# Linear attention and MLP on one core: two loads of tokens issued sooner, one GpSimd subtraction held back behind a norm, and one tile's sums in another order

## The chip, the core and the metric

The kernel runs on one core of a Trainium2 chip. The metric is the device time of one execution in microseconds (us); lower is better. TensorE (PE) multiplies matrices, VectorE (DVE), ScalarE (ACT) and GpSimd (POOL) work element by element, and SyncE (SP) issues nearly all DMAs, in the order in which they stand in the program. An engine works through its own instructions strictly in order, and so does SP: an instruction that waits holds up all that stand behind it.

## The reference

```
xn  = layernorm(x)                               x: 2048 x 512, float32
qkv = xn @ wqkv                                  32 heads of 16
pq, pk = phi(q), phi(k)                          phi(t) = (t + 1 if t > 0 else exp(t)) + 1e-6
kv  = sum over tokens of pk^T v,  z = sum over tokens of pk
o   = (pq kv) / (pq z + 1e-6)
A   = o @ wo
B   = relu(xn @ w1 + b1)^2 @ w2 + b2             hidden size 1376
out = x + A + B
```

## The kernel before, in words

The 2048 tokens are 16 tiles of 128. All matrix products are kept near float32 by splitting each operand into a high part (rounded to float32r) and a low part (the rest), and by three passes: high by high, high by low, low by high.

The first stage goes over the tiles in order. For tile `i`:

- `load_x` (line 157) brings its rows of x. Tiles 0 to 3 come singly, 4 to 7 with one DMA, 8 to 15 in pairs of 512 KB each. The buffers of tiles 12 and 13 are those of tiles 0 and 1 (`two("x12")`), those of 14 and 15 are those of 2 and 3.
- `measure` (L230, L231) takes mean and variance on VectorE, `roots` (L241, L242) makes the reciprocal root on GpSimd with a power (the tile `power` holds the exponent), and `normalise` writes the normalised tile `xp`: on VectorE (L264) for tiles 0 to 7, on ScalarE (L254) from tile 8 on.
- The tile has to be transposed for the projection. Tiles 0 to 3 are transposed on TensorE (L304). From tile 4 on it goes through memory: `regroup` (line 273) stores `xp` to a buffer `via` (L277) as soon as the tile is normalised, and appends four gathers to the list `moves`; `move` (L285) issues them, which brings `xg`; then VectorE's block transpose (L289) finishes the turn. Tiles 4 and 5 have a `via` and a gather each (`xg4s`, 256 KB), later tiles go in pairs (512 KB).
- ScalarE makes the high part of the transposed tile (L320), VectorE the low part (L323). For tiles up to 7 the transposed tile is also kept in memory (`xTd`, L332).
- `project` (L365) multiplies it by the key weights: 12 matmuls into the bank `pk`. `phi_k` applies phi (ScalarE L356 and L358, VectorE L360), and `parts` splits the result (ScalarE L111 for the high part, VectorE L373 for the low one). `tokens` splits the normalised tile itself into `tok` (ScalarE L111 high, GpSimd L119 low).
- `kx` (L385) adds tokens times keys into four banks: 12 matmuls, three passes of four. Its order is a table by tile: for the first tiles high tokens by high keys, then low tokens by high keys, then high tokens by low keys; from tile 2 on the low tokens come last.

Tiles 0 to 3 are written out by hand, line by line (lines 515 to 649), with the loads of tiles 8 to 11 placed behind tile 2's steps. The loop over `i` from 2 to 15 (line 788 on) then issues, per turn: the gathers in `moves`; in turn 2 the loads of tiles 12 to 15; in turns 4 and 7 a copy of a block of transposed tiles to memory (`xsd`, two DMAs of 1 MB, L802); the projection of tile `i`; phi; the norm of the tiles two or more ahead with its `via`; the splits; the statistics further ahead; and last `kx(i - 1)`. So on TensorE the order is projection of tile 3, sums of tile 2, projection of tile 4, sums of tile 3, and so on.

For tiles 0 to 2 the order on the other engines is by hand too. Around the change VectorE does: phi of tile 0 (L360), statistics of tile 4, low keys of tile 0 (L373), phi of tile 1, norm of tile 4 (L264), statistics of tile 5, low keys of tile 1 (L373), then the low part of tile 3 (L323) and so on. GpSimd does: low tokens of tile 0 (L119), root of tile 4 (L241, L242), low tokens of tile 1 (L119), root of tile 5. SP does: `xTd` of tiles 0 and 1, loads of 8/9 and 10/11, `via` of tile 4, `xTd` of tile 2, four gathers of tile 4, loads of 12/13 and 14/15, `via` of tile 5, `xTd` of tile 3, four gathers of tile 5, `via` of tiles 6 and 7, `xTd` of 4 and 5, four gathers of 6 and 7, and the two copies of 1 MB.

After this stage the values and the query projection are folded into matrices, and two large rounds of matmuls follow (L130, L484), which take most of the time.

Of the kernel before, what the change touches and what calls it, by code (L numbers as in the profile page):

```python
# [7 lines left out]
F32 = mybir.dt.float32  # L8
# [5 lines left out]
P = 128  # L14
# [4 lines left out]
def kernel(  # L19
# [30 lines left out]
    nc = tc.nc  # L50
# [21 lines left out]
    keep = ctx.enter_context(tc.tile_pool(name="keep", bufs=1))  # L72
# [8 lines left out]
    def w512(name, tag, bufs):  # L81
        return work.tile([P, 512], F32, name=name, tag=tag, bufs=bufs)
# [3 lines left out]
    def next_tag(of):  # L86
        k, n = turns[of]
        turns[of][0] = (k + 1) % n
        return f"{of}{k}"

    def two(name):
        return keep.tile([P, 2, 512], F32, name=name, tag=next_tag("x"))
# [4 lines left out]
    def pair(name):  # L97
        return keep.tile([P, 2, 512], F32R, name=name, tag=next_tag("pair"))

    def f32(ap):  # L100
        return ap.bitcast(F32)

    def gjc(ap):

        return ap.rearrange("p (j g c) -> p g j c", j=NJ, g=NJ)
# [3 lines left out]
    def copy(eng, o, i, bias=0.0):  # L109
        if eng == "act":  # L110
            nc.scalar.activation(o, i, AF.Copy, bias=bias)  # L111
        elif bias:
            ENG[eng].tensor_scalar(o, i, bias, None, op0=OP.add)
        else:
            ENG[eng].tensor_copy(o, i)

    def split(h, l, src, eh, el):
        copy(eh, h, src)
        ENG[el].tensor_tensor(out=l, in0=src, in1=f32(h), op=OP.subtract)  # L119
# [30 lines left out]
    heads = work.tile([P, P], F32, name="heads", tag="heads")  # L150
    b1s = keep.tile([P, NF], F32, name="b1s")
    zc = keep.tile([P, 2, NJ], F32, name="zc")
    power = keep.tile([P, 3], F32, name="power")

    xr, xp, xg, tok, pk, kp = {}, {}, {}, {}, {}, {}

    def load_x(i, t):
        n = t.shape[1]
        nc.sync.dma_start(t, xf[i * P:(i + n) * P, :].rearrange("(i p) d -> p i d", i=n))
        for k in range(n):  # L160
            xr[i + k] = t[:, k]
# [82 lines left out]
    def normalise(tiles, st, mv, y):  # L244

        n = len(tiles)
        r, u = (y[:, k, :n] for k in range(2))
        if tiles[-1] >= NPE:

            nc.vector.scalar_tensor_tensor(u, mv[:, :n, 0], -1.0, r, op0=OP.mult, op1=OP.mult)  # L250
        later = []

        def last(i, o, src, k):
            nc.scalar.activation(o, src, AF.Identity, bias=u[:, k:k + 1], scale=r[:, k:k + 1])  # L254
            if i in groups:
                regroup(i)

        for k, i in enumerate(tiles):
            o, src = xp[i], xr[i]
            if i >= NDVE:  # L260

                o, src = o.rearrange("p g (j c) -> p g j c", j=NJ), gjc(src)
            if i < NPE:
                nc.vector.tensor_scalar(o, src, mv[:, k, 0:1], r[:, k:k + 1], op0=OP.subtract, op1=OP.mult)  # L264
                if i in groups:
                    regroup(i)
            else:
                later.append(lambda a=(i, o, src, k): last(*a))
        return later
# [3 lines left out]
    def regroup(i):  # L273

        src, G = groups[i]
        via = dram.tile([P, NJ, src.shape[-1]], F32, name=f"via{i}")
        nc.sync.dma_start(via, src)  # L277
        of_g = via.rearrange("(r t) g n -> g t r n", r=NJ)
        for g in range(NJ):
            moves.append((G[32 * g:32 * (g + 1)], of_g[g]))  # L280
# [11 lines left out]
    def slot(i):  # L292
        return slice((i % TB) * P, (i % TB + 1) * P)

    def cols(i):

        return xsb[(i // TB + 1) % 2]
# [42 lines left out]
    def ones(i):  # L340

        nc.gpsimd.memset(xp[i][:, D - 1:] if i < NDVE else xp[i][:, NJ - 1, P - 1:], 1.0)

    def tokens(i):
        tok[i] = pair(f"tok{i}")
        h, l = tok[i][:, 0], tok[i][:, 1]
        src = xp[i]
        if i >= NDVE:
            h, l, src = gjc(h), gjc(l), src.rearrange("p g (j c) -> p g j c", j=NJ)
        split(h, l, src, "act", "pool")  # L350
        if NDVE <= i + 1 < NT:
            ones(i + 1)
# [9 lines left out]
    def project(i, ps, w, steps, first=True, last=True):  # L362

        for n, (j, u, v) in enumerate(steps):
            nc.tensor.matmul(ps, lhsT=cols(i)[u][:, j, slot(i)], rhs=w[v][:, j, :], start=first and n == 0,  # L365
                             stop=last and n == len(steps) - 1)

    def parts(i):

        p = kp[i]  # L370
        pk[i] = pair(f"pk{i}")
        copy("act", pk[i][:, 0], p, 1e-6)
        nc.vector.scalar_tensor_tensor(pk[i][:, 1], p, 1e-6, f32(pk[i][:, 0]), op0=OP.add, op1=OP.subtract)  # L373

    def phi_k(i, ps, mid=lambda: None, late=lambda: None):
        kp[i] = w512(f"k{i}", "p", 6)
        phi(ps, kp[i], mid, late)

    def kx(i):
        second, third = ((1, 0), (0, 1)) if i < 2 else ((0, 1), (1, 0))  # L380
        order = (((1, 0),), ((0, 0), (0, 1))) if i >= NPE else (((0, 0),), (second,), (third,))
        todo = [(c, u, v) for group in order for c in range(NJ) for u, v in group]
        first, last = order[0][0], order[-1][-1]
        for c, u, v in todo:
            nc.tensor.matmul(kxp[c], lhsT=tok[i][:, u, c * P:(c + 1) * P], rhs=pk[i][:, v],  # L385
                             start=i == 0 and (u, v) == first, stop=i == NT - 1 and (u, v) == last)
# [152 lines left out]
    for i0 in range(0, NT, TB):  # L539
# [6 lines left out]
        if i0 < NPE:  # L546
            single = work.tile([P, 2, 512], F32, name=f"xg{i0}s", tag="r0")
            for k in range(2):
                i = i0 + k
# [3 lines left out]
        for k in range(0, n, 2):  # L553
            i = i0 + TB - n + k
# [51 lines left out]
    third = statistics(2)  # L606
# [25 lines left out]
    rest(3)  # L632
    load_x(8, x8[:, :2])
    load_x(10, x8[:, 2:])
    project(2, pks[2], wk, HL)
    single = group(4)
    soon = group(5)
# [4 lines left out]
    roots(*single)  # L642
    parts(0)
    phi_k(1, pks[1])
    tokens(1)
    normalise(*single)
    measure(soon)
    parts(1)
    roots(*soon)
    keep2()  # L650

# [137 lines left out]
    for i in range(2, NT):  # L789
        if i == 13:  # L790
            nc.sync.dma_start(b1s[:, :NF - 1], b1[:(NF - 1) * P].rearrange("(f p) -> p f", p=P))
            for a, o, n in units(NF - 1):
                nc.sync.dma_start(b1s[a:a + n, NF - 1:], b1[o:o + n, None])
        move()
        if i == 2:
            load_x(12, two("x12"))
            load_x(14, two("x14"))
        if i in (4, 7):

            b = i // 7  # L800
            for u in range(2):
                nc.sync.dma_start(xsd[b][u], f32(cols(b * TB)[u]))  # L802
        if i >= 8:
            fetch()
        ps = pks[i] if i < 3 else bank(f"pk{i}")
        if i > 2:
            project(i, ps, wk, HL)
        high = low = keep_t = lambda: None
        if i < NDVE:
            high, low, keep_t = transposed(i + 1)  # L810

        soon_turned = transposed(i + 2) if 11 <= i and i + 2 < NT else ()

        def mid():
            high()
            more(i)

        def late():
            low()
            more(i)  # L820

        if i == 12:
            rawz = raw_1(NF - 1)
            T.update({n: tokens_sum(n, f"B{n - 1}") for n in (1, 2)})
        if i == 12:
            w = load_1("q", 0)
        if i == 13:
            todo_1 = operands_first(0, w)
            extra.append(todo_1.pop(1))
        if i == 14:  # L830
            z = pair("w1z0")
            extra.append(lambda: split(z[:, 0], z[:, 1], rawz, "act", "dve"))
            o34 = halves(four("Tf", "r0"))
            extra.extend(sums_of(xT[NB - 1], xT[NB - 2], *o34))
            lows = [extra.pop() for k in range(2)]
            extra += [todo_1[0], lows[1], todo_1[1], lows[0], *todo_1[2:]]
        phi_k(i, ps, mid, late)
        more(i)
        run(*soon_turned)
        later = normalise(*soon) if soon else []  # L840
        parts(i)
        keep_t()
        if i == 2:
            tokens(2)
        if i + 1 < NT:
            tokens(i + 1)
        run(*later)
        if NDVE < i + 2 < 13:
            run(*transposed(i + 2))
        pieces([3, 1, 1, 2, 1][i - 11] if i > 10 else 0)  # L850
        if i == 2:
            ahead[3] = statistics(6, 7)
        if i + 2 in (4, 6, 8, 10):
            ahead[i + 2] = group(i + 6, i + 7)
        if i < 10:
            measure(ahead[(i + 2) // 2 * 2], i % 2)
        soon = ahead.get(i + 1, ())
        if soon:
            roots(*soon)
        kx(i - 1)  # L860
        more(i)

# [477 lines left out]
```

## Time and profile before

| | before |
|---|---|
| runs shown | 418.06 us median of 3 (417.35 to 418.07) |
| the profiled execution | 418.47 us |
| its span, first to last instruction | 416.8 us |
| TensorE busy | 409.1 us, 98% |
| VectorE, ScalarE, GpSimd busy | 312.7, 264.5 and 59.2 us |

The profile is of one execution. A row of the timeline gives start, duration, engine, line, operation, written tile<-read tiles, sizes and how many instructions are merged; in square brackets stands how long the engine had been idle before it, and what ended that. Rows merged from several instructions overlap a little with the next, as matmuls are pipelined. A row of the chain of work that ended last gives start, duration and what ran or was waited for. A row of the DMA issues gives written<-read, the queue, how many, the size of one, and the us from issue to landing. Rows of the windows give the busy time of each engine in a stretch, the granted TensorE clock (1.00 is full speed), the share of DMA engines busy, and GB/s.

### The profile page before, as it was taken

What the parts mean: (1) busy time and instruction counts of PE and PEld (TensorE: products, weight loads), DVE (VectorE), ACT (ScalarE), POOL (GpSimd) and SP (SyncE); (2) the same over time, 40 slices, a digit from 0 to 9 for tenths busy, and PEclk for the clock granted to TensorE, in tenths of its full rate; (3) what the DMA queues carried; (4) which work ended last, traced back from release to release, by engine and by line L of the source; (5) the groups of instructions that cost most, each with busy time, mean ns of one, the idle gap of its engine ahead of it and who ended that gap; (6) DMA issues with size and microseconds to landing.
All of it is one profiled execution on the core that took longest, in us unless ns stands there. A gap on an engine that the chain in (4) does not pass through costs nothing.

```text
span 416.8 us, 5402 instructions
## 1 busy us (share of the span) xinstructions
PE 409.1 (98%) x1827; PEld 337.7 (81%) x1827; DVE 312.7 (75%) x556; ACT 264.5 (63%) x464; POOL 59.2 (14%) x93
## 2 busy tenths in 40 slices
PE   8997999999999999999999999999999999999996
PEld 7885888888888888888878888888888888878885
DVE  5983676799699898997539996477998685449843
ACT  4754677664687788889555731467678857737420
POOL 5552233121140000020000040100000200000210
PEclk9998999999999999999999999999999999999999
DMA  6777867740321212355176991511231781025602
GB/s 207 251 209 250 293 238 240 224 109 1 102 76 52 76 51 77 101 159 94 35 294 236 336 256 56 152 52 29 60 89 27 223 181 50 2 85 166 103 0 101
DMA packets 46381, 55.67 MB, mean 134 GB/s; under 512 B 8081, under 2 KB 30353, under 8 KB 45074
## 3 DMA queue, kind: packets, MB, share of 16 engines
q1 hardware_dynamic: 44050, 51.14, 38.0%
q0 software_dynamic: 2304, 4.20, 6.1%
q8 instruction: 14, 0.23, 0.2%
q14 instruction: 13, 0.11, 0.1%
HBM read 41.69 MB, written 13.63 MB: 133 GB/s over the span
## 4 chain that ended last, share of the span: by engine, by line
PE 92%; DMA 3%; DVE 2%; ACT 1%; POOL 1%; issue 0%; SPq 0%; DVEq 0%
PE acc L130 37%; PE b L484 32%; PE pk L365 9%; PE kx L385 8%; PE acc L495 2%; DMA via<-xp 1%; PE pz L130 1%; PE pkv L891 1%; DVE st L230 1%; DMA x<-in_A_x_dram 1%; PE pm L130 1%; PE pz0b L130 1%; PE b L130 1%; DVE xp L264 1%; DMA xg4s<-via 0%
## 5 line engine op out<-in xcount | busy, mean ns | idle before, releaser
L130 PE MATMUL acc<-w2r,s 128*128 128x512 f32 x477 | 112.8, 390 | 0.0
L130 PEld LDWEIGHTS acc<-w2r,s 128*128 128x128 f32 x477 | 89.4, 188 | 19.3 <-issue 0.7
L484 PE MATMUL b<-T,aop 128*128 128x512 f32 x336 | 83.4, 389 | 0.0
L484 PEld LDWEIGHTS b<-T,aop 128*128 128x128 f32 x336 | 63.0, 188 | 13.2
L385 PE MATMUL kx<-pk,tok 128*128 128x512 f32 x192 | 46.4, 391 | 0.0
L385 PEld LDWEIGHTS kx<-pk,tok 128*128 128x128 f32 x192 | 36.1, 189 | 7.8 <-ACT pk L111 0.2
L1021 POOL DMA_DIRECT2D res<-in_B_b_dram x16 | 14.4, 1116 | 181.8 <-DVE w2r L122 63.2
L484 PE MATMUL b<-xs0h,aop 128*128 128x512 f32 x112 | 36.9, 390 | 0.0
L130 PE MATMUL acc<-mh,aTsr 128*128 128x512 f32 x112 | 35.6, 389 | 0.0
L1029 DVE TENSOR_TENSOR res<-acc,res 128x512 f32<-128x512 f32 x16 | 11.0, 692 | 23.0 <-PE acc L130 18.3
L119 POOL TENSOR_TENSOR tok<-xp,tok 128x512 fp32r<-128x512 f32 x16 | 20.8, 1305 | 39.3 <-ACT tok L111 39.3
L122 DVE TENSOR_TENSOR w2r<-r,w2r 128x512 fp32r<-128x512 f32 (+2 forms) x35 | 25.6, 733 | 0.1
L484 PEld LDWEIGHTS b<-xs0h,aop 128*128 128x128 f32 x112 | 21.0, 188 | 4.4
L130 PEld LDWEIGHTS acc<-mh,aTsr 128*128 128x128 f32 x112 | 21.0, 188 | 4.4
L111 ACT ACTIVATE aop<-S 128x512 fp32r<-128x512 f32 x28 | 17.4, 623 | 10.6 <-DVE S L716 10.6
L119 DVE TENSOR_TENSOR aop<-S,aop 128x512 fp32r<-128x512 f32 x28 | 19.5, 697 | 4.8 <-ACT aop L111 4.4
L119 DVE TENSOR_TENSOR s<-c,s 128x512 fp32r<-128x512 f32 x20 | 13.6, 689 | 11.5 <-ACT s L111 11.5
L130 PE MATMUL acc<-ml,aTsr 128*128 128x512 f32 x56 | 21.8, 389 | 0.0
L484 PE MATMUL b<-xs0l,aop 128*128 128x512 f32 x56 | 21.8, 389 | 0.0
L111 ACT ACTIVATE w2r<-r 128x512 fp32r<-128x512 f32 x32 | 19.6, 619 | 2.6 <-DMA out_dram<-res 2.0
L111 ACT ACTIVATE T<-Tf 128x512 fp32r<-128x512 f32 x16 | 9.5, 625 | 16.4 <-DVE Tf L659 16.3
L484 PE MATMUL b<-xs1h,aop 128*128 128x512 f32 x56 | 19.5, 389 | 0.0
(194 smaller groups left out, 773.4 us busy)
## 6 DMA issues: line engine op xcount, KB each, us to landing
r<-in_B_w_dram SPq DMA_DIRECT2D x49, 256.0 KB, 3.1
res<-in_A_x_dram SPq DMA_DIRECT2D x8, 512.0 KB, 4.3
res<-in_B_b_dram POOLq DMA_DIRECT2D x16, 256.0 KB, 5.7
out_dram<-res SPq DMA_DIRECT2D x15, 256.0 KB, 2.1
via<-xp SPq DMA_DIRECT2D x5, 512.0 KB, 6.3
xg<-via SPq DMA_DIRECT2D x20, 128.0 KB, 3.0
xTd<-t SPq DMA_DIRECT2D x8, 256.0 KB, 4.0
x<-in_A_x_dram SPq DMA_DIRECT2D x4, 512.0 KB, 5.8
```

The lines of the kernel that those rows point to most:

```text
L111: nc.scalar.activation(o, i, AF.Copy, bias=bias)
L119: ENG[el].tensor_tensor(out=l, in0=src, in1=f32(h), op=OP.subtract)
L122: nc.vector.tensor_tensor(out=l, in0=src, in1=f32(h), op=OP.subtract)
L130: nc.tensor.matmul(ps, lhsT=a[u], rhs=b[v], start=first and n == 0, stop=last and n == 2)
L230: nc.vector.bn_stats(st[:, k, :], xr[tiles[k]])
L264: nc.vector.tensor_scalar(o, src, mv[:, k, 0:1], r[:, k:k + 1], op0=OP.subtract, op1=OP.mult)
L365: nc.tensor.matmul(ps, lhsT=cols(i)[u][:, j, slot(i)], rhs=w[v][:, j, :], start=first and n == 0, stop=last and n == len(steps) - 1)
L385: nc.tensor.matmul(kxp[c], lhsT=tok[i][:, u, c * P:(c + 1) * P], rhs=pk[i][:, v], start=i == 0 and (u, v) == first, stop=i == NT - 1 and ( ...
L484: nc.tensor.matmul(ps, lhsT=a[u][:, j * P:(j + 1) * P], rhs=b[v][:, j, :], start=first and j == 0 and n == 0, stop=last and j == 1 and n == 2,
L495: nc.tensor.matmul(ps, lhsT=s[u][:, k * P:(k + 1) * P], rhs=w2s[NF - 1][u][:, a:z], start=first and u == 0, stop=stop and u == 1)
L1021: nc.gpsimd.dma_start(r[:, i], b2[None, :].partition_broadcast(P), accum_op=OP.add)
L1029: nc.vector.tensor_tensor(out=r[:, a:z], in0=ps, in1=r[:, a:z], op=OP.add)
```

## The change

Four edits, all in the first stage:

```diff
-    power = keep.tile([P, 3], F32, name="power")
+    power = keep.tile([P, 4], F32, name="power")
...
     def kx(i):
-        second, third = ((1, 0), (0, 1)) if i < 2 else ((0, 1), (1, 0))
+        second, third = ((1, 0), (0, 1)) if i < 1 else ((0, 1), (1, 0))
...
     rest(3)
     load_x(8, x8[:, :2])
     load_x(10, x8[:, 2:])
+    load_x(12, two("x12"))
     project(2, pks[2], wk, HL)
...
     roots(*single)
     parts(0)
     phi_k(1, pks[1])
+    normalise(*single)
+    load_x(14, two("x14"))
+    nc.gpsimd.tensor_copy(power[:, 3:], xp[4][:, 0, :1])
     tokens(1)
-    normalise(*single)
+    parts(1)
     measure(soon)
-    parts(1)
     roots(*soon)
     keep2()
...
         move()
-        if i == 2:
-            load_x(12, two("x12"))
-            load_x(14, two("x14"))
```

- On SP the load of tiles 12 and 13 now stands right behind that of 10 and 11, ahead of the `via` of tile 4; the load of 14 and 15 stands between the `via` of tile 4 and the `xTd` of tile 2. Behind the gathers of tile 4 the `via` of tile 5 follows at once. Nothing else on SP changes.
- On GpSimd a copy of one column of the normalised tile 4 into an unused column of `power` stands ahead of the low tokens of tile 1. It reads what the norm of tile 4 writes, so GpSimd doesn't start those low tokens before that norm is done. GpSimd runs one instruction more than before (87 after 86).
- On VectorE the low keys of tile 1 (L373) now stand ahead of the statistics of tile 5; the number of instructions stays 538.
- The sums of tile 1 take low keys second and low tokens third, as those of tile 2 and later do. The number of matmuls is the same.

## The prediction

> **What bounds the kernel now.** I read the list of waits of TensorE first, then its timeline around the one long stop, then the chain that led to it.
>
> ```profile
> PE 409.1 (98%) x1827; PEld 337.7 (81%) x1827; DVE 312.7 (75%) x556; ACT 264.5 (63%) x464; POOL 59.2 (14%) x93
> ```
> ```profile
> PE pk L365 <- ACT xs0h L320: 2.8, 1, 2.8
> ```
> ```profile
> 30.88 2.88 PE L385 MATMUL kx<-pk,tok 128*128 128x512 f32 x12
> 36.52 0.50 PE L365 MATMUL pk<-wkh,xs0h 128*128 128x512 f32 x1 [2.75 <-ACT xs0h L320]
> 40.92 3.00 PE L385 MATMUL kx<-pk,tok 128*128 128x512 f32 x12
> 43.76 0.39 PE L365 MATMUL pk<-wkh,xs0h 128*128 128x512 f32 x1
> ```
> ```profile
> 43.92 2.72 PE pk L365 x12
> 46.64 2.72 PE kx L385 x12
> ```
> ```profile
> 39.00:40.00 1.00, 1.00 (x3) 0.79 (x3) 0.84 (x2) 1.00 (x3) 0.26 (x2) 0.50 0.77 208
> ```
>
> TensorE is busy 98% of the span, so only its stops and its clock can give time back. There is one long stop, ahead of tile 5's projection (36.52). An undisturbed tile takes 2.72 + 2.72 = 5.44 us. Without a stop the sums of tile 3 end at 30.88 + 2.72 = 33.60, tile 5's projection follows, then the sums of tile 4 (36.32), and tile 6's projection starts at 33.60 + 5.44 = **39.04**. It starts at 43.76: **4.72 us** late. Of these 36.52 - 33.60 = 2.92 are the stop, and 43.76 - 36.52 - 5.44 = 1.80 are slow matmuls, since the granted clock falls to 0.50 after the stop (the third column from the right). From there TensorE runs without a wait, so what is saved by 43.76 reaches the end.
>
> Why tile 5 is late, in the chain and the order of SP:
>
> ```profile
> 25.88 5.73 DMA via<-xp
> 32.96 1.94 DMA xg4s<-via
> 35.09 0.72 DVE t L289
> ```
> ```profile
> 11.74 1.91 SPq L159 DMA_DIRECT2D x<-in_A_x_dram  x2
> 19.85 0.34 SPq L277 DMA_DIRECT2D via<-xp  x1
> ...
> 23.09 1.76 SPq L285 DMA_DIRECT2D xg4s<-via  x4
> 24.89 0.94 SPq L159 DMA_DIRECT2D x<-in_A_x_dram  x2
> 25.88 0.47 SPq L277 DMA_DIRECT2D via<-xp  x1
> ...
> 31.63 1.76 SPq L285 DMA_DIRECT2D xg4s<-via  x4
> 33.49 0.38 SPq L277 DMA_DIRECT2D via<-xp  x1
> 33.91 2.44 SPq L332 DMA_DIRECT2D xTd<-t  x2
> 36.45 2.03 SPq L285 DMA_DIRECT2D xg<-via  x4
> ```
> ```profile
> via<-xp SPq DMA_DIRECT2D x1, 256.0 KB, 3.2
> ```
> ```profile
> via<-xp SPq DMA_DIRECT2D x1, 256.0 KB, 5.7
> ```
>
> The two loads at 24.89 (12 to 15, 1 MB) stand just ahead of the via of tile 5. That via (second DMA row) takes 5.7 us to land; tile 4's, of the same size with no load ahead of it (first row), takes 3.2. While SP waits for it (to 31.63), the via of tiles 6 and 7 stands behind it too and is issued at 33.49, though its data was ready:
>
> ```profile
> 18.29 1.54 DVE L264 TENSOR_SCALAR xp<-x,mv,y 128x512 f32<-128x512 f32 x1
> 22.33 0.54 DVE L264 TENSOR_SCALAR xp<-x,mv,y 128x512 f32<-128x512 f32 x1
> 26.58 0.71 DVE L289 STREAM_TRANSPOSE t<-xg4s 128x512 f32<-128x512 f32 x1 [0.37 <-DMA xg4s<-via]
> 29.20 0.99 DVE L264 TENSOR_SCALAR xp<-x,mv,y 128x512 f32<-128x512 f32 x2
> 41.79 0.71 DVE L289 STREAM_TRANSPOSE t<-xg 128x512 f32<-128x512 f32 x1 [1.79 <-DMA xg<-via]
> ```
>
> Norms 6 and 7 end at 29.20 + 0.99 = 30.19.
>
> **The change, part by part.**
>
> *Norm of tile 4.* It takes 1.54 us where tile 5's takes 0.54.
>
> ```profile
> 15.66 1.30 POOL L119 TENSOR_TENSOR tok<-xp,tok 128x512 fp32r<-128x512 f32 x1 [0.97 <-ACT tok L111]
> 18.24 1.30 POOL L119 TENSOR_TENSOR tok<-xp,tok 128x512 fp32r<-128x512 f32 x1
> 8.60 0.18 POOL L592 COPY x<-xp 128x1 f32<-128x1 f32 x1
> ```
>
> GpSimd's low tokens of tile 1 run from 18.24 to 19.54, and the norm ends just behind them. With GpSimd waiting for it, the norm should take about 0.55 and end at 18.84, so the via of tile 4 goes out at 18.86 in place of 19.85: 1.0 us sooner. GpSimd pays one copy (0.18), starts the low tokens at about 19.1 and ends them at 20.4.
>
> *Loads.* The load of 12/13 goes out behind the two at 11.74, near 13.65. DMA at that time:
>
> ```profile
> 16.00:17.00 1.00, 1.00 (x6) 0.73 (x5) 0.96 (x3) 0.98 (x2) 1.00 (x2) 1.00 1.05 404
> 18.00:19.00 1.00, 1.00 (x6) 0.78 (x5) 1.00 (x2) 0.76 (x3) 0.99 (x2) 1.00 0.00 0
> ```
>
> The engines move 404 GB/s and are empty from 18 on, so 512 KB more is done 1.3 us later, near 19, as the via starts; I cost it at nothing. The load of 14/15 goes out right behind that via. Its cost is not shown: between nothing (3.2 us, the via being first in the queue) and half of what 1 MB ahead cost tile 5's via, (5.7 - 3.2) / 2 = 1.25. I take 3.2, as the via is ahead, and keep 1.25 for the range.
>
> *The new sequence*, each step with its old distance:
> - Via of 4 lands at 18.86 + 3.2 = 22.1; gathers until 22.1 + 1.76 = 23.9. The turn came 26.58 - 23.09 = 3.5 after the first gather: 25.6. VectorE's own queue ahead of the turn was done at 26.58 - 0.37 = 26.2 and starts from a norm that ends 1.0 sooner, of which the low keys' wait for ScalarE and the root of tile 5 give back most: I estimate 25.9 and take that. Tile 4's projection starts 36.52 - 35.09 = 1.43 behind a turn: 27.3. Its place is 30.88 - 2.72 = 28.16: no stop.
> - Via of 5 (norm 5 was done at 22.33 + 0.54 = 22.87) goes out at 23.9, lands at 27.1; turn at 27.1 + (35.09 - 31.63) = 30.6, projection ready at 32.0, place 33.60. The stop is gone with 1.6 to spare, and the slow clock with it.
> - What is late next: tile 6. Norms 6 and 7 keep 29.20 - 26.58 = 2.62 behind turn 4: 28.5 to 29.5. SP is free at 27.1 + 1.76 = 28.9, so via 6/7 goes out at 29.5, 4.0 sooner; its gathers come 36.45 - 33.49 = 2.96 later, 32.5; the turn 41.79 - 36.45 = 5.34 behind them, 37.8; ready at 39.25, place 39.04. A stop of **0.2** stays.
>
> ```profile
> 45.32 0.63 ACT L111 ACTIVATE pk<-k 128x512 fp32r<-128x512 f32 x1 [1.00 <-DVE k L360]
> 51.82 0.71 DVE L289 STREAM_TRANSPOSE xT<-xg 128x512 f32<-128x512 f32 x1 [0.33 <-DMA xg<-via]
> ```
>
> - The sums of tile 5 then start 1.43 + 2.72 = 4.15 behind turn 6, and its high keys end 45.32 + 0.63 - 41.79 = 4.16 behind it: about **0.1** more. Tile 8, ready at 51.82 + 1.43 = 53.25, has its place at 43.76 + 10.88 = 54.64, 1.4 to spare; gathers that move 3.9 against matmuls that move 4.4 leave 0.9.
>
> *Sums of tile 1 and VectorE's order.*
>
> ```profile
> 19.78 3.02 PE L385 MATMUL kx<-pk,tok 128*128 128x512 f32 x12
> ```
> ```profile
> 18.40 0.63 ACT L111 ACTIVATE pk<-k 128x512 fp32r<-128x512 f32 x1 [0.24 <-DVE k L360]
> ```
> ```profile
> 16.56 0.94 DVE L373 SCALAR_TENSOR_TENSOR pk<-k,pk 128x512 fp32r<-128x512 f32 x1
> 20.56 0.66 DVE L373 SCALAR_TENSOR_TENSOR pk<-k,pk 128x512 fp32r<-128x512 f32 x1
> ```
>
> The second pass starts at 19.78 + 0.91 = 20.69, the third at 21.6. Low tokens last (20.4, at worst 21.1) are in time. Low keys (L373) are now second: their high part is there at 19.03, so 19.1 + 0.66 = 19.8, in time, unless GpSimd holds them up. The row at 16.56 took 0.94 and ended 0.54 behind GpSimd's low tokens (16.96). Here both want to start at 19.1. If GpSimd is first, L373 ends at 20.4 + 0.54 = 20.95, and TensorE stops 0.3. If VectorE is first, the low tokens end at about 21.1. I take VectorE, by a hair.
>
> The Trainium skill (SBUF — State Buffer, section "SBUF: two separate sides") speaks against the change here: the pair of ports that VectorE and GpSimd share is an exclusive lock for a whole instruction, and a VectorE operation with two SBUF inputs takes it against a GpSimd one that reads SBUF. The rows at 18.29 and 16.56 agree; by it the norm's 1.0 us isn't removed but partly handed to the low keys, which is the second case below.
>
> **Sum.** 4.72 - 0.2 - 0.1 = 4.4; with the via at the late end (1.25) tile 4 stops 0.3, tile 6 is ready at 40.3, and the gain is 3.4. I take **4.2**, near the early end. The profiled execution would go from 418.47 (0.4 above the median, 1.7 of it around the span of 416.8) to 414.3, the median from 418.06 to **413.9**.
>
> **Rivals.**
> - *The low tokens win the lock* (or the norm stays long, so that the change doesn't do what it says; the via then goes 1.0 later): 0.3 of stop in tile 1's sums, then VectorE's queue is 20.95 - 19.8, some 1.1, later up to turn 4, via 6/7 goes out at 30.5, tile 6 is ready at 40.2 and the gain is 43.76 - 40.2 - 0.1 = 3.4: **414.7**. For it: the copy is short (0.18). Against: GpSimd starts behind a wait.
> - *The clock falls again*, after the short stop at tile 6: the 1.80 comes back, gain 2.4, **415.7**. For it: one stop of 2.75 was enough. Against: this one is 0.2 to 1.2. The Trainium skill (TensorE: Matmul & The Clock Gate, section "Why this matters for your kernels") asks for no idle gaps above about 3 us, so by it this doesn't happen; but 2.75 sufficed here.
> - *Tile 8 doesn't move*, because the 2 MB of copies behind gathers 6/7 hold the queue: 4.2 less 1.4 to spare is lost, gain 1.4, **416.7**. Against: these copies are issued behind the same gathers, which move.
> - *Slower:* the via of tile 4 is caught between the loads of 12/13 and 14/15. TensorE then stops at tile 4, and the clock halves there. It loses the whole 4.72 from a stop of 4.72 - 1.80 = 2.9 on, which is a landing 7.2 us after the issue (28.16 + 2.9 - 1.43 - 3.5 = 26.1). At 8.0 the time is **418.9**. Against: 1 MB ahead gave 5.7.
>
> **How the numbers follow.** Forecast 0.50; lock or norm (414.7) 0.25; clock 0.10; tile 8 0.06; via 4 caught 0.09, of which 0.04 near its break-even and 0.05 beyond. The range: from no stop at all (418.06 - 4.72 = 413.3, less 0.3 of scatter) to the clock's case: 413.0 to 415.8, about 0.85. A measurement tells about 0.2% from no change. Faster 0.91, same 0.04, slower 0.05.
>
> **What would show it.** Norm 4 near 0.55; vias of 4 and 5 landing in about 3.2; via 6/7 issued near 29.5; no stop ahead of tile 5; granted clock 1.00 throughout 31 to 45; a stop of some tenths ahead of tile 6's projection, which starts near 39.3. Wrong if L373 of tile 1 ends near 21, if the first via lands above 4.5, or if a stop of over 1 us stands anywhere behind.

## The result, and the profile after

The changed kernel takes **414.27 us** (median of 5 runs, 414.23 to 414.67) where the kernel before takes 418.07 in the same comparison (417.35 to 418.38): a ratio of **0.9913**, 95% interval 0.9898 to 0.9927, 3.8 us less. In the profiled executions it is 414.27 after 418.47. In a later comparison the ratio was 0.9932 (0.9919 to 0.9944), 414.92 after 417.81. Every run of this document has the kernel before beside it on the same chip; runs of different comparisons are set against each other by their ratios. By the profiles GpSimd runs 94 instructions after 93, and VectorE 556 in both; the counts given with the change (87 after 86, and 538) are lower, with the same difference.

TensorE's waits and its timeline in the changed kernel:

```profile
PE pk L365 <- ACT xs0h L320: 0.3, 1, 0.3
```
```profile
19.49 3.27 PE L385 MATMUL kx<-pk,tok 128*128 128x512 f32 x12
...
30.77 2.88 PE L385 MATMUL kx<-pk,tok 128*128 128x512 f32 x12
33.49 0.39 PE L365 MATMUL pk<-wkh,xs0h 128*128 128x512 f32 x1
...
39.35 0.50 PE L365 MATMUL pk<-wkh,xs0h 128*128 128x512 f32 x1 [0.27 <-ACT xs0h L320]
...
44.98 0.39 PE L365 MATMUL pk<-wkh,xs0h 128*128 128x512 f32 x1
```

The stop ahead of tile 5's projection (2.8 us before) is gone: it starts at 33.49, where the sums of tile 3 end. What is left is 0.27 ahead of tile 6's, and a new one of 0.25 inside the sums of tile 1 (12 matmuls from 19.49 in 3.27 us, 3.02 before). Tile 7's projection starts at 44.98, before at 49.20: 4.2 us sooner, and that is what the profiled execution gains. By the medians it is 3.8, and 2.9 in the later comparison.

SP's queue, the landings and VectorE:

```profile
18.58 0.34 SPq L277 DMA_DIRECT2D via<-xp  x1
18.98 0.43 SPq L159 DMA_DIRECT2D x<-in_A_x_dram  x1
...
21.18 1.80 SPq L285 DMA_DIRECT2D xg4s<-via  x4
23.07 0.38 SPq L277 DMA_DIRECT2D via<-xp  x1
...
25.99 1.73 SPq L285 DMA_DIRECT2D xg4s<-via  x4
30.03 0.34 SPq L277 DMA_DIRECT2D via<-xp  x1
...
33.69 1.73 SPq L285 DMA_DIRECT2D xg<-via  x4
```
```profile
x<-in_A_x_dram SPq DMA_DIRECT2D x1, 512.0 KB, 4.9
via<-xp SPq DMA_DIRECT2D x1, 256.0 KB, 2.5
```
```profile
xg4s<-via SPq DMA_DIRECT2D x2, 64.0 KB, 3.4
```
```profile
via<-xp SPq DMA_DIRECT2D x1, 256.0 KB, 2.9
```
```profile
18.01 0.54 DVE L264 TENSOR_SCALAR xp<-x,mv,y 128x512 f32<-128x512 f32 x1
18.80 1.80 DVE L373 SCALAR_TENSOR_TENSOR pk<-k,pk 128x512 fp32r<-128x512 f32 x1 [0.24 <-ACT pk L111]
...
26.39 0.71 DVE L289 STREAM_TRANSPOSE t<-xg4s 128x512 f32<-128x512 f32 x1
...
29.01 1.00 DVE L264 TENSOR_SCALAR xp<-x,mv,y 128x512 f32<-128x512 f32 x2
...
30.52 0.70 DVE L289 STREAM_TRANSPOSE t<-xg4s 128x512 f32<-128x512 f32 x1
...
37.93 0.71 DVE L289 STREAM_TRANSPOSE t<-xg 128x512 f32<-128x512 f32 x1 [2.52 <-DMA xg<-via]
```
```profile
18.62 0.19 POOL L648 COPY power<-xp 128x1 f32<-128x1 f32 x1 [0.72 <-DVE xp L264]
18.76 1.29 POOL L119 TENSOR_TENSOR tok<-xp,tok 128x512 fp32r<-128x512 f32 x1
```

Read down the rows: the norm of tile 4 takes 0.54 (1.54 before); its via lands in 2.5 us with a 512 KB load right behind it; the gathers behind that load land in 3.4 (1.9 before); the via of tile 5 lands in 2.9 (5.7 before); VectorE turns tile 5 at 30.52 with no idle time ahead (35.09 before, after 4.3 us of waiting). And the low keys of tile 1 (L373) take 1.80 in place of 0.66: GpSimd's low tokens started at 18.76, 0.04 us ahead of them.

### The profile page after: what moved, and what is told of

It is laid out like the page before. It is cut to its first block, busy times and chain, and to the rows that moved or that the text cites. A ratio compares the mean times of both kernels' runs of the same rounds, so it can differ in the third digit from the quotient of the medians.

```text
span 412.5 us, 5402 instructions
## 1 busy us (share of the span) xinstructions
PE 407.1 (99%) x1827; PEld 336.0 (81%) x1827; DVE 312.7 (76%) x556; ACT 264.7 (64%) x464; POOL 59.2 (14%) x94
## 4 chain that ended last, share of the span: by engine, by line
PE 90%; DVE 4%; DMA 2%; ACT 1%; POOL 1%; issue 1%; SPq 0%; DVEq 0%
PE acc L130 37%; PE b L484 32%; PE kx L385 7%; PE pk L365 7%; PE acc L495 2%; PE pz L130 1%; DVE st L230 1%; DMA via<-xp 1%; PE pkv L891 1%; DMA xg<-via 1%; PE pm L130 1%; DMA x<-in_A_x_dram 1%; PE pz0b L130 1%; PE b L130 1%; DVE k L360 1%; DVE pk L373 1%
```

## The experiments

The theory to be tried: the 1 MB of loads ahead of tile 5's via made the stop, moving them makes nearly all of the gain, the norm adds some tenths, and from 30 to 39 us it is tile 6's way through memory, no longer TensorE, that sets the end. Rivals: the held-back low tokens make the gain; or the halved clock was a loss of its own.

**1. The loads alone.**

```diff
     load_x(10, x8[:, 2:])
+    load_x(12, two("x12"))
...
     tokens(1)
     normalise(*single)
+    load_x(14, two("x14"))
     measure(soon)
     parts(1)
...
-        if i == 2:
-            load_x(12, two("x12"))
-            load_x(14, two("x14"))
```

> Only the two loads are moved (12/13 behind 10/11, 14/15 behind the via of tile 4); GpSimd's low tokens, VectorE's order and the order of the sums are those of before. My theory (the loads make the gain, the norm adds some tenths): norm 4 takes 1.5 us again, its via goes out at 19.5 and lands near 22.1, gathers behind 14/15 take 3.4 us, turn of tile 4 near 27.0 and a stop of about 0.5 ahead of its projection; tile 5 has no stop and the clock stays at 1.00; tile 6 starts near 40.0. Time about 414.9. Rival (the held-back low tokens make the gain): 417 or more.

Measured: 415.07, ratio 0.9931 (0.9915 to 0.9947). In the profile, norm 4 took 1.54, its via went out at 19.79, tile 4's projection stopped 0.34 and tile 6's started at 39.85. So the loads alone make some 0.7% of the 0.7 to 0.9%, and the rest of the change adds 0.0 to 0.2%, which these intervals don't part from nothing. The profiled execution itself was 416.38, since there one of the late gathers came last (the first row is of TensorE, the second of the chain):

```profile
74.12 0.50 PE L365 MATMUL pk<-wkh,xs0h 128*128 128x512 f32 x1 [1.25 <-ACT xs0h L320]
```
```profile
59.49 8.87 DMA via<-xp
```

That is the via of tiles 12 and 13, behind 2 MB of copies and the loads of `wo`; in the changed kernel tile 12 is turned at 70.34 and projected from 72.18 on, so it has 72.18 - 70.34 - 1.43 = 0.4 us to spare. It didn't stop TensorE in the other profiles but one (0.34 us in experiment 6).

**2. The hold and the orders alone**: the changed kernel with the two loads back in turn 2.

```diff
-    load_x(12, two("x12"))
...
-    load_x(14, two("x14"))
...
+        if i == 2:
+            load_x(12, two("x12"))
+            load_x(14, two("x14"))
```

> The loads stay where they were before; GpSimd's copy, VectorE's order and the sums' order are those of the changed kernel. My theory: norm 4 takes 0.54 and its via goes out 1 us sooner, but the via of tile 5 stands behind 1 MB again and takes about 5.7 us to land; a stop of about 1.5 us ahead of tile 5 and one of about 1.3 ahead of tile 6; time 416.1 if the clock stays at 1.00, 416.6 or more if it halves after the first stop. Rival (the held-back low tokens make the gain): 415 or less.

Measured: 416.51, ratio 0.9959 (0.9944 to 0.9974), near the theory's 416.1; the two stops are 1.11 and 0.73, where 1.5 and 1.3 were expected. The timeline of TensorE and of SP:

```profile
34.93 0.50 PE L365 MATMUL pk<-wkh,xs0h 128*128 128x512 f32 x1 [1.11 <-ACT xs0h L320]
...
41.48 0.50 PE L365 MATMUL pk<-wkh,xs0h 128*128 128x512 f32 x1 [0.73 <-ACT xs0h L320]
```
```profile
23.03 0.94 SPq L159 DMA_DIRECT2D x<-in_A_x_dram  x2
24.02 0.47 SPq L277 DMA_DIRECT2D via<-xp  x1
24.59 0.53 SPq L332 DMA_DIRECT2D xTd<-t  x1
30.03 1.75 SPq L285 DMA_DIRECT2D xg4s<-via  x4
```

The sooner norm moves the whole queue by 1 to 2 us, but the via of tile 5 still takes 6.0 us (24.02 to 30.03) behind 1 MB. The rival that the hold makes the gain falls: the time is far from 415. Still, the hold and the orders by themselves save 1.5 us. That doesn't add to what the loads save, since both bring tiles 5 and 6 sooner: tile 6 starts at 41.48 here, at 39.85 with the loads alone and at 39.35 with both (43.76 before).

**3. The old order of tile 1's sums**, in the changed kernel.

```diff
-        second, third = ((1, 0), (0, 1)) if i < 1 else ((0, 1), (1, 0))
+        second, third = ((1, 0), (0, 1)) if i < 2 else ((0, 1), (1, 0))
```

> The changed kernel, but the sums of tile 1 take the low tokens second as before. Theory (from 30 to 39 us the way of tile 6 through memory sets the end, and a stop ahead of it costs nothing): the low tokens are there at 20.05, so the stop of 0.25 in tile 1's sums goes, but the stop ahead of tile 6 grows by as much, and the time stays within 0.1 of the changed kernel's 414.3. Rival (TensorE is the bound throughout, and the order of the sums carries its stop to the end): 414.0. Rival (the old order needs the low tokens sooner than they are there): above 414.5.

Measured: 414.96, ratio 0.9923 (0.991 to 0.9937). The stop in tile 1's sums is gone (12 matmuls in 3.00 us), and the one ahead of tile 6 is 1.01, but the time is 0.6 above what was expected: the gathers of tiles 6 and 7, issued at 33.83, were followed by the turn at 38.72, 4.9 us later, where the changed kernel's took 4.2. To see whether that belongs to the order, both kernels were run side by side on another chip:

> The changed kernel itself, run on the same chip as the next three so that they can be compared directly. 414.3 as before, if the 0.5 to 0.7 by which the old order of the sums came out slower belongs to that kernel; near 414.9 if it was this chip's DMA (the gathers of tiles 6 and 7 came 4.9 us before the turn there, 4.2 in the changed kernel's profile).

> The old order of tile 1's sums once more, beside the changed kernel. Theory (the way of tile 6 through memory sets the end, what is saved in tile 1's sums is waited for ahead of tile 6): within 0.2 of the changed kernel in the same call. Rival (the order of the sums costs by itself): 0.5 or more slower than it, rival (its stop of 0.25 reaches the end): 0.25 faster.

Measured: 414.92 (0.9932) for the changed kernel and 414.61 (0.993, 0.9917 to 0.9944) for the old order. They are the same within their scatter. In these two profiles it is the changed kernel whose turn of tile 6 comes late (38.58, a stop of 0.59) and the old order's that comes sooner (37.72, 0.20). From the gathers to the turn these two profiles take about the same (4.55 and 4.50); what differs is that the old order's execution was some 0.4 ahead from tile 1 on, and that its via of tiles 6 and 7 took 3.2 us to its gathers and not 3.7. So the order of tile 1's sums is worth nothing that can be measured, either way: the way of tiles 6 and 7 through memory scatters more (3.2 to 3.7 us from via to gathers, 4.2 to 4.9 from gathers to turn, over these four profiles). That a stop in tile 1's sums is always made up ahead of tile 6 fits the profiles, but is not shown beyond this scatter.

**4. The low keys first**: GpSimd waits for them and not for the norm.

```diff
-    nc.gpsimd.tensor_copy(power[:, 3:], xp[4][:, 0, :1])
-    tokens(1)
+    tok[1] = pair("tok1")
+    copy("act", tok[1][:, 0], xp[1])
     parts(1)
+    nc.gpsimd.tensor_copy(power[:, 3:], f32(pk[1][:, 1, :1]))
+    nc.gpsimd.tensor_tensor(out=tok[1][:, 1], in0=xp[1], in1=f32(tok[1][:, 0]), op=OP.subtract)
```

> The changed kernel, but GpSimd's copy reads the low keys of tile 1, so that VectorE's L373 takes the lock first and the low tokens follow. Theory: L373 takes 0.66 and not 1.80, the low tokens end near 20.9, ahead of the third pass at 21.3, no stop in tile 1's sums. VectorE reaches the turn of tile 4 some 1 us sooner, but then waits for the gathers (near 26.0, 0.35 sooner); via 6/7 goes out at 29.65 and tile 6 starts near 39.0: 413.9. Rival (via 6/7 doesn't follow VectorE, or lands no sooner): 414.3, unchanged.

Measured: **413.41**, ratio 0.9889 (0.987 to 0.9908). VectorE, GpSimd, SP and TensorE of its profile:

```profile
18.80 0.69 DVE L373 SCALAR_TENSOR_TENSOR pk<-k,pk 128x512 fp32r<-128x512 f32 x1 [0.25 <-ACT pk L111]
...
25.59 0.71 DVE L289 STREAM_TRANSPOSE t<-xg4s 128x512 f32<-128x512 f32 x1
```
```profile
19.56 0.18 POOL L651 COPY power<-pk 128x1 f32<-128x1 f32 x1 [1.66 <-DVE pk L373]
19.70 1.30 POOL L652 TENSOR_TENSOR tok<-xp,tok 128x512 fp32r<-128x512 f32 x1
```
```profile
29.23 0.34 SPq L277 DMA_DIRECT2D via<-xp  x1
...
32.43 1.73 SPq L285 DMA_DIRECT2D xg<-via  x4
```
```profile
38.71 0.39 PE L365 MATMUL pk<-wkh,xs0h 128*128 128x512 f32 x1
```

The low keys take 0.69, tile 4 is turned 0.8 sooner than in the changed kernel, the via of tiles 6 and 7 goes out 0.8 sooner, and tile 6 has no stop at all: TensorE runs from tile 2 on without a wait. The time is 0.5 below what I expected. In the same comparison the loads alone had 0.9931 and the old order of the sums 0.9923, and this version's interval lies below both of theirs. Run again on another chip:

> The kernel whose low keys go first, once more, on whatever chip it gets. If its lead over the changed kernel (413.4 after 414.3 and 414.9) is its own, the ratio to the kernel before stays near 0.989 and the profile shows no stop or at most 0.3 us ahead of tile 6; if it was a lucky landing of the gathers of tiles 6 and 7, the ratio is 0.991 to 0.993, as the changed kernel's, and a stop of 0.5 to 1.0 stands ahead of tile 6.

Measured: 413.88, ratio 0.9898 (0.988 to 0.9916), again with no stop ahead of tile 6. This version is the fastest that was found; its two ratios lie below both of the changed kernel's. The intervals overlap with that of the changed kernel's first comparison, and lie below that of the later one.

**5. The long stop filled**, in the kernel before: 11 extra matmuls, whose result the projection overwrites.

```diff
+        if i == 5:
+            for _ in range(11):
+                nc.tensor.matmul(ps, lhsT=cols(4)[0][:, 0, slot(4)], rhs=wk[0][:, 0, :], start=True, stop=True)
         if i > 2:
             project(i, ps, wk, HL)
```

> The kernel before, with 11 extra matmuls (2.5 us) of data already there ahead of tile 5's projection, into its own bank, which the projection then starts anew: the long stop is filled, so that the clock doesn't fall. The prediction's sum put 1.80 of 4.72 us to the slow clock. If that is a loss by itself: 416.2. Theory from the runs since: without the slow clock TensorE is ready for tile 6 at 42.0, but tile 6 is ready only 1.43 behind its turn (41.79), at 43.2 in place of 43.76, so at most 0.5 is saved: 417.4 or more.

Measured: 418.16 after 418.10, ratio 0.9997 (0.9982 to 1.0011): no saving shows, and the interval allows for 0.8 us at most, so the 1.80 is not a loss of its own. Its TensorE and VectorE:

```profile
33.14 2.65 PE L808 MATMUL pk<-wkh,xs0h 128*128 128x512 f32 x11
...
42.39 0.50 PE L365 MATMUL pk<-wkh,xs0h 128*128 128x512 f32 x1 [0.72 <-ACT xs0h L320]
```
```profile
40.97 0.71 DVE L289 STREAM_TRANSPOSE t<-xg 128x512 f32<-128x512 f32 x1 [1.64 <-DMA xg<-via]
```

The granted clock is 1.00 throughout, tile 5's matmuls run at full speed, and then TensorE waits 0.72 for tile 6, which comes 42.39 - 40.97 = 1.42 behind its turn (and later 0.28 for tile 8). In the kernel before, tile 6 was ready at 41.79 + 1.42 = 43.21 and started at 43.76. So of the 1.80 of slow matmuls at most 0.55 was lost; the rest only filled that wait.

**6. Both loads ahead of the via of tile 4.**

```diff
     load_x(12, two("x12"))
+    load_x(14, two("x14"))
...
-    load_x(14, two("x14"))
```

> The changed kernel, but both loads stand ahead of the via of tile 4. This tries the slower case of the prediction (that via caught behind the loads). Theory: the load of 14/15 goes out near 15, all loads are through near 20, the via at 18.6 lands near 22.4 and not 21.2, but its gathers have nothing ahead of them and take 1.9 and not 3.4 us; turn of tile 4 near 26.4 either way: 414.3, as the changed kernel. If the via were caught badly (landing above 24): 416 or more.

Measured: 415.19, ratio 0.9936 (0.9922 to 0.995). The via of tile 4 and TensorE's first stop:

```profile
via<-xp SPq DMA_DIRECT2D x1, 256.0 KB, 4.7
```
```profile
28.45 0.50 PE L365 MATMUL pk<-wkh,xs0h 128*128 128x512 f32 x1 [0.42 <-ACT xs0h L320]
```

The via takes 4.7 us and not the 3.8 expected, its gathers 2.0, and tile 4 stops 0.42: a little of the slower case is real, but far from its break-even of 7.2. By time it can't be told from the changed kernel beside it (0.9932). VectorE and GpSimd of the same profile:

```profile
18.85 0.69 DVE L373 SCALAR_TENSOR_TENSOR pk<-k,pk 128x512 fp32r<-128x512 f32 x1 [0.20 <-ACT pk L111]
```
```profile
18.86 1.84 POOL L119 TENSOR_TENSOR tok<-xp,tok 128x512 fp32r<-128x512 f32 x1
```

Here VectorE came first, by 0.01 us: its low keys take 0.69, GpSimd's low tokens take 1.84 in place of 1.29, and tile 1's sums don't stop. In the six other profiles with this order of VectorE and GpSimd, the low tokens were 0.04 ahead, and the low keys took 1.79 or 1.80.

**7. One load.** The changed kernel with the load of 14/15 back ahead of the via of tile 5.

```diff
-    load_x(14, two("x14"))
...
+        if i == 2:
+            load_x(14, two("x14"))
```

> The changed kernel, but the load of 14/15 stays in its old place ahead of the via of tile 5; only 12/13 goes out early. Theory: 512 KB ahead cost that via about 1.2 us, half of what 1 MB cost, so it lands in 4.1; turn of tile 5 near 31.9, ready at 33.3, just in time for its place near 33.5; via 6/7 goes out at 30.0 or a few tenths later; the time is within 0.5 of the changed kernel's. If tile 5 still stops by over 1 us (the load costs as a whole and not by its bytes): 416.

Measured: 414.13, ratio 0.9922 (0.9908 to 0.9936). The via of tile 5 took 4.2 us, tile 5 was turned at 31.25 and did not stop. With no load, 512 KB and 1 MB just ahead of it that via takes 2.9, 4.2 and 5.7 us, about 1.4 for each 512 KB; in other profiles it takes 2.1 to 3.6 with none, 4.5 with 512 KB, and 5.5 and 6.0 with 1 MB. Each load is one DMA of 512 KB, so the runs don't part the bytes from the number of loads. Half of the move is enough: the changed kernel beside it had 0.9932.

**8 and 9. The low keys first, with the load of 14/15 elsewhere**: behind the gathers of tile 5, or in its old place.

```diff
-    load_x(14, two("x14"))
...
+        if i == 3:
+            load_x(14, two("x14"))
```

> As the kernel whose low keys go first, and the load of 14/15 stands behind the gathers of tile 5, where the DMA engines are empty. Theory: the gathers of tile 4 land in 1.9 and not 3.4 us, tile 4's turn then follows VectorE alone (near 25.4); no stop is left to be taken away, so the time is that of the kernel with the low keys first, 413.4, within 0.3. Rival (the load then meets the via of 6/7, which lands later): a stop ahead of tile 6 and 413.9 or more.

> As the kernel whose low keys go first, but the load of 14/15 stays ahead of the via of tile 5 as in the kernel before. Theory: the via of tile 5 lands in 4.2, its turn near 31.2, ready at 32.6, place 33.3; via 6/7 waits for the gathers of tile 5 until 29.5 and tile 6 is ready near 38.7: 413.4, within 0.3 of the kernel with the low keys first. If tile 6 stops: 413.8 or more.

(For the second of them, the condition reads `i == 2`.) Measured: 414.26 (0.9908, 0.9889 to 0.9928) and 414.51 (0.9915, 0.9893 to 0.9938). Here my expectation failed, and the rival of the first came out. SP and TensorE of the first:

```profile
27.16 0.43 SPq L159 DMA_DIRECT2D x<-in_A_x_dram  x1
29.27 0.34 SPq L277 DMA_DIRECT2D via<-xp  x1
...
33.64 1.74 SPq L285 DMA_DIRECT2D xg<-via  x4
```
```profile
39.91 0.50 PE L365 MATMUL pk<-wkh,xs0h 128*128 128x512 f32 x1 [0.95 <-ACT xs0h L320]
```

The via of tiles 6 and 7 goes out at 29.27, as in experiment 4 (29.23), but its gathers can follow only at 33.64, 4.4 us later and not 3.2. In the other profiles with both loads early that takes 3.2 to 3.7, so a load issued 2.1 us ahead of it, which lands only after 3.7, still costs it 0.7 to 1.2 us. In the second, SP waits for the via of tile 5 (4.5 us), and via 6/7 goes out at 30.03; tile 6 stops 0.81. These two ran on a third chip, and their intervals overlap with those of experiment 4; it is the stops in their profiles that show the loss.

## Why the prediction was right

- *The stop ahead of tile 5 and its cause.* Right: experiments 1, 2 and 7 show that the loads ahead of the via made it, and that half of them makes about half of the delay.
- *Norm of tile 4.* Right: 0.54, via 1.3 us sooner (1.0 forecast; VectorE was 0.3 ahead in this execution). With the loads moved, the hold and the orders together add nothing that experiment 1 can tell from zero, since the low keys then pay for the norm; without the moved loads they save 1.5 us (experiment 2).
- *Loads at no cost, via of tile 4 in 3.2 us.* The via took 2.5 with a load behind it, and the gathers behind that load took 3.4 and not 1.9. I had put the whole risk on the via and none on the gathers. It did no harm here: the turn of tile 4 came at 26.39 in place of 25.9, but VectorE has no idle time ahead of it, so VectorE's queue set it, with the long low keys in it, and not the gathers (experiment 4, whose low keys are short, turns tile 4 at 25.59 behind gathers that take 3.8). The Trainium skill (DMA: Bandwidth & Descriptors, section "Queues, rings and completion order") says that each DMA engine takes a queue's descriptors in ring order; both rows agree with it.
- *What is late next: tile 6, with 0.2 and 0.1.* Right: 0.27, and tile 7 is at 44.98 where 39.25 + 5.44 + 0.1 = 44.8 was forecast. But the size is luck. Three terms of it were off against each other: via 6/7 went out at 30.03 (29.5 forecast), took 3.7 us to its gathers (2.96), and from there to the turn 4.2 (5.34). A second profile of the same kernel has 0.59 in place of 0.27.
- *"I take VectorE, by a hair."* Wrong. GpSimd was first by 0.04 us, L373 took 1.80 and ended at 20.60, and tile 1's sums stopped 0.25, as the rival "the low tokens win the lock" had it; an end near 21 was also one of the prediction's own signs of being wrong. In this profile that rival's price was too high: VectorE's delay at turn 4, against experiment 4, was 0.8 and not 1.1, via 6/7 went out at 30.03 and not at 30.5, and from there the turn followed in 7.9 us and not in 8.3; tile 6 started at 39.35 and not at 40.2, so the gain was 4.2 and not 3.4. Over all runs it was not: the rival's 414.7 is a ratio of 0.992, which lies in both intervals of the changed kernel (0.9898 to 0.9927 and 0.9919 to 0.9944), while the forecast's 413.9 is 0.990, inside the first only by its lower end and outside the second. So the sequence came as forecast but for the lock, where the rival held, and the median near 413.9 is in part luck.
- *The sum's 1.80 for the slow clock.* The step was wrong as an explanation, though the total of 4.72 wasn't: experiment 5 takes the slow clock away and no saving shows, as TensorE then waits for tile 6, which still comes 1.4 behind its turn. The kernel before itself has runs with and without it: in one comparison four of 11 runs had a granted clock of 1.00 over the span (417.63 to 418.08), seven had 0.992 to 0.996 (417.27 to 419.4).
- *The rivals.* The clock didn't fall behind the short stops (0.999 over the span), and not behind stops of 1.11 and 0.73 in experiment 2. Tile 8 had its 0.9 to spare. Via 4 was caught a little with both loads ahead of it (4.7 us), nowhere near 7.2.

## What to carry to other kernels

A store that a gather waits for shouldn't have large loads ahead of it in the same queue: put them where the DMA engines are empty and nothing on the path follows soon, and count what stands behind them, not only the next transfer. (Whether loads in another queue would spare the store was not tried.) When a stop is taken away, work out at once which arrival is late next; the slow clock behind a stop may only be filling the next wait. And where two engines lock each other out, as these rows show, and both come at nearly the same time, don't leave the order to some hundredths: let the one on the path go first with a wait; here that version was the fastest.

## What the runs showed of the hardware that I had not expected

- A clock that halves after a stop doesn't do so in every run. Some executions of the kernel before have a granted clock of 1.00 over the span, though only one of its executions left a trace, so how long the stop was in those isn't known. In its profile the slow stretch is 3.4 us long by these windows (the clock is the third column from the right):

```profile
37.00:38.00 1.00, 1.00 (x6) 0.76 (x5) 0.96 (x4) 0.61 (x1) 0.00 (x0) 0.81 1.01 286
...
41.00:42.00 1.00, 1.00 (x6) 0.81 (x5) 0.21 (x1) 0.20 (x1) 0.18 (x2) 0.98 1.03 434
```

With 0.50 in the three windows between, that is 0.38 + 3 + 0.04 us at half clock. The Trainium skill (TensorE: Matmul & The Clock Gate, section "What's actually happening") describes a free-running window of about 3.4 us over which activity is judged; whether a stop of 2.75 falls mostly into one window or across two might explain both, if a window that is idle only in part can count; no run here shows the window itself.

- Gathers with the same queue ahead of them came up to 0.7 us apart (4.2 us from issue to turn in the changed kernel, 4.9 in experiment 3, where only the order of TensorE's sums differs), more than the smaller parts of this change are worth; two profiles of the changed kernel showed stops of 0.27 and 0.59 ahead of tile 6.
